# Masks on VectorE, casts off GpSimd, a written-out order for the first stages, DMA transposes of the last local q and k, and a last store in halves

## The chip, the cores and the metric

The kernel runs on one core of one Trainium2 chip. A core has TensorE (matrix products and transposes, which write PSUM), VectorE, ScalarE and GpSimd, and 16 DMA engines that are fed by queues on SyncE (SP) and GpSimd. Each engine works through its own instructions strictly in the order in which the program wrote them, and waits for other engines by semaphores. The metric is the device time of one execution in microseconds (us).

## The reference

Two layers, one after the other. The first is an attention over 8 batches, 8 heads, 576 positions and 64 columns a head:

```python
scores = scale * (q @ k.T)                   # per batch and head
mask_local   = (rel >= 0) & (rel < 32)       # heads 0 to 3, rel = row - column
mask_strided = (rel >= 0) & (col % 32 == row % 32)   # heads 4 to 7
attn = softmax(where(mask, scores, -1e9)); x = attn @ v   # -> [4608, 512]
```

The second is a feed-forward layer on the 4608 rows of x:

```python
h = x @ w_in                                 # [4608, 512] @ [512, 2048]
g = maximum(h, 0) + alpha * minimum(h, 0)    # alpha: one value a column
out = g @ w_out                              # [4608, 2048] @ [2048, 512]
```

All inputs and the output are float32; inside, the kernel works in float16 with float32 sums.

## The kernel before

**Attention.** The masks leave few scores alive, so only blocks are computed. Heads go in pairs, four pairs to a batch: pairs 0 and 1 (called a, b here) are local, six windows of 96 rows against 128 keys; pairs 2 and 3 (A, B) are strided, eight groups of 72 rows. The work of a pair is cut into pieces. **T** (`transpose_piece`, line 233) turns q or k of two pairs on TensorE, eight 128x128 transposes into PSUM, and ScalarE (for batches 0 and 1 ScalarE and VectorE) copies the result into `qT`, `kT`. **S** (`score_both`, line 388; `score_early` and `score_piece` for batches 0 and 1) computes the scores in two halves, i = 0 and 1; ScalarE takes the exponential into a tile `et`, and the mask is applied. **P** (`pv_piece`, line 435) multiplies with v, where a column of ones gives the softmax's sum; VectorE takes the reciprocal (line 458) and scales (line 460). **X** (`x_piece`, `x_dma`, `x_copy`) turns the result into `xT`, a ring of three batches.

**Masks.** For batches 0 and 1 an additive mask `madd` is added to the scores by a matrix product with the identity, before the exponential (lines 320 and 366). From batch 2 on the exponential is multiplied by a 0/1 mask on GpSimd (lines 423 and 430).

**Local q and k** come as float32, are cast by `cast_l` (GpSimd for batches 0 to 2, ScalarE for 3 to 7) and turned on TensorE. Strided q and k of batches 2 to 7 are turned by DMA transposes from `qsd`, `ksd` (`transpose_d`, line 132, on SP's queue).

**Feed-forward.** Rows go in nine chunks of 512 (n = 0 to 8). `lin1_piece(n, m)`, line 619, makes 128 of the 2048 columns: four products, then ScalarE's `neg` (line 639) and VectorE's combination into `gT` (line 641). It uses one of three PSUM buffers `hps`, so TensorE can run only three pieces ahead of VectorE. Chunk 0 uses the plain second product (`lin2_piece`, line 740). Chunks 1 to 8 use `fast_piece` (line 674), a two-by-two scheme with seven products P1 to P7, each in two pieces; it needs sums of quarters of `gT` (`g_sums`, on VectorE, line 647) and of `w_out` (`w_sums`). The last product, P3, completes a quadrant of 256 rows by 256 columns, which one addition and one store write out.

**Order.** Batch 0 runs alone at the start, between dummy products `warm` that keep TensorE busy. Then come the sixteen lin1 pieces of chunk 0, then its sixteen lin2 pieces with batch 1's attention pieces between them, and then chunks 1 to 8: each has 16 lin1 and 14 fast pieces, and attention pieces of a later batch are put between them, by the list `PACE1` for chunk 1 and by an even share for the others. The second half of a pair's exponentials is held back (`defer`) and issued one attention step later. GpSimd's queue carries all loads with a cast, in program order with its masks, casts and copies; SP's queue carries the stores, the later loads of local q and k, and all DMA transposes.

Of the kernel before, what the change touches and what calls it, by code (L numbers as in the profile page):

```python
# [31 lines left out]
def kernel(  # L32
# [21 lines left out]
    SUM1 = {8.5: [0], 18.5: [2], 19.0: [1, 3, 5], 20.5: [4], 22.0: [7], 24.5: [6]}  # L54
    PACE1 = (0, 1, 0, 0, 1, 0, 1, 0, 0, 0, 1, 1, 0, 1, 0, 1, 1, 1, 1, 2, 1, 1, 2, 0, 1, 2, 0, 1, 1, 1)
    SUMS = {10: [(0, LOW)], 16: [(1, LOW)], 17: [(0, HIGH)], 18: [(1, HIGH)],
            20: [(2, LOW)], 21: [(2, HIGH)], 23: [(3, LOW)], 25: [(3, HIGH)]}

# [49 lines left out]
    def load_qk(b, strided, nm):  # L108

        h0 = 4 if strided else 0
        src = q if nm == "q" else k
        if strided and b:
            t16 = hpool.tile([128, 2, 512], F16, tag=f"{nm}s", bufs=2, name=f"{nm}s")
            cast16[(b, True, nm)] = t16
        else:
            t16 = hpool.tile([128, 2, 512], F32, tag=f"{nm}l", bufs=2, name=f"{nm}l")
            loaded[(b, strided, nm)] = t16
        base = src[b, h0 : h0 + 1, 0:1, :]  # L120
        eng = nc.sync if (b > 2 and not strided) or (b == 0 and strided) else nc.gpsimd
        keep(eng.dma_start(t16, bass.AP(
            tensor=base.tensor, offset=base.offset,
            ap=[[8 * D, 64], [2 * S * D, 2], [S * D, 2], [1, 8 * D]])))
# [13 lines left out]
    def cast_s(b, nm, eng):  # L138
        t16 = hpool.tile([128, 2, 512], F16, tag=f"{nm}s", bufs=2, name=f"{nm}s")
        if eng[0] == eng[1]:  # L140
            cast_copy(eng[0], t16, loaded[(b, True, nm)])
        else:
            for f in range(2):
                cast_copy(eng[f], t16[:, f : f + 1, :], loaded[(b, True, nm)][:, f : f + 1, :])
        cast16[(b, True, nm)] = t16
# [20 lines left out]
    def load_v(b, strided):  # L166
# [8 lines left out]
        else:  # L175
            v16 = vls[b % 2]
            base = v[b, 0:1, 0:1, :]
            r0 = 32 if b < 2 else 0
            keep(nc.gpsimd.dma_start(
                v16[r0:128, :, 0:64],  # L180
                bass.AP(tensor=base.tensor, offset=base.offset - (32 - r0) * D,
                        ap=[[D, 128 - r0], [96 * D, 24], [1, D]])))
# [18 lines left out]
    def over_v(b, eng):  # L201

        v16 = vls[b % 2]
        cast_copy(eng, v16[0:32, 1:24, :], v16[96:128, 0:23, :])
# [6 lines left out]
    wide = {"on": True}  # L211
    NEARLY = 2

# [19 lines left out]
    def transpose_piece(u, nm):  # L233
# [6 lines left out]
        early = b < NEARLY  # L240
        src = cast16[(b, strided, nm)]
# [12 lines left out]
        if early:  # L254
            for e in range(2):
                eng = "dve" if (nm == "q") == (e == 0) else "act"
                if u == 0 and nm == "q":
                    eng = "act"
# [5 lines left out]
        if nm == "k":  # L264
            tails(b, u, strided)

    def tails(b, u, strided):
# [11 lines left out]
        qeng = "dve" if b < NEARLY else "act"  # L279
        for i, (o, eng) in enumerate(((qTs[u % 2][:, :, 0:576], qeng), (kTs[u % 2][:, :, 32:608], "act"))):  # L280
# [9 lines left out]
    def score_early(P):  # L290
# [3 lines left out]
        for i in range(2):  # L294
# [8 lines left out]
            n = w * len(grp)  # L303
            for x, t in enumerate(grp):
                k0 = 32 + 72 * t if P.strided else 96 * t
                for y in range(2):
# [3 lines left out]
                        P.qT[hf, w * t : w * t + w], start=(x == 0), stop=False, skip_group_check=True))  # L310
                    P.et[(2 * (t // 2) + y, t % 2) if P.strided else (t, y)] = (et, n * y + w * x)
            todo.append((i, et[0:r, 0 : 2 * n], sps, n))
        for i, ev, sps, n in todo:
            if not P.strided and i == 0:
                m = madd[:, 0:288]
            else:
                m = madd[0:72, 288:360] if P.strided else madd[:, 96:192]
                m = m.unsqueeze(1).to_broadcast([r, n // w, w])
            for y in range(2):
                keep(nc.tensor.matmul(  # L320
                    sps[y][:, 0:n], ident[0:r, :], m, start=False, stop=True, skip_group_check=True))
            if i == 0:
                keep(nc.scalar.activation(
                    ev.rearrange("r (y c) -> r y c", y=2), sp[0:r, :, 0:n], AF.Exp, scale=SCALE))
                continue
            for y in range(2):
                keep(nc.scalar.activation(
                    ev[:, n * y : n * y + n], sps[y][0:r, 0:n], AF.Exp, scale=SCALE))

    def score_piece(P, i):  # L330

        et = ets[ectr["i"] % NE]
        if wide["on"] and ectr["i"] % 2:
            sps = [phpool.tile([128, 512], F32, tag="hps", name="sph") for _ in range(2)]
        else:
            sp = pbpool.tile([128, 2, 512], F32, tag="sp", name="sp")
            sps = [sp[:, y] for y in range(2)]
        ectr["i"] += 1
        w, grp = P.w, P.sgroups[i]
        n = w * len(grp)  # L340
        r = 72 if P.strided else 128
        early = P.b < NEARLY
        for x, t in enumerate(grp):
            if P.dx:
                q0 = k0 = 80 * (4 * (2 * P.pr + t % 2) + t // 2)
            else:
                q0, k0 = w * t, 32 + 72 * t if P.strided else 96 * t
            for y in range(2):
                hf = slice(64 * y, 64 * y + 64)
                keep(nc.tensor.matmul(  # L350
                    sps[y][:, w * x : w * x + w], P.kT[hf, k0 : k0 + 128],
                    P.qT[hf, q0 : q0 + w], start=(x == 0),
                    stop=(x == len(grp) - 1 and not early), skip_group_check=True))

                key = (2 * (t // 2) + y, t % 2) if P.strided else (t, y)
                P.et[key] = (et, n * y + w * x)
        first = not P.strided and i == 0
        if early:

            if first:  # L360
                m = madd[:, 0:288]
            else:
                m = madd[0:72, 288:360] if P.strided else madd[:, 96:192]
                m = m.unsqueeze(1).to_broadcast([r, n // w, w])
            for y in range(2):
                keep(nc.tensor.matmul(
                    sps[y][:, 0:n], ident[0:r, :], m, start=False, stop=True, skip_group_check=True))
        ev = et[0:r, 0 : 2 * n]
        if wide["on"] and ectr["i"] % 2 == 0:
            for y in range(2):  # L370
                keep(nc.scalar.activation(
                    ev[:, n * y : n * y + n], sps[y][0:r, 0:n], AF.Exp, scale=SCALE))
        else:
            keep(nc.scalar.activation(
                ev.rearrange("r (y c) -> r y c", y=2), sp[0:r, :, 0:n], AF.Exp, scale=SCALE))
        if early:
            return
        if first:
            ev = ev.rearrange("r (y c) -> r y c", y=2)
            m = mfirst.unsqueeze(1).to_broadcast([r, 2, n])  # L380
        else:
            ev = ev.rearrange("r (c f) -> r c f", f=w)
            m = (mstr if P.strided else mother).unsqueeze(1).to_broadcast([r, 2 * n // w, w])
        keep(nc.gpsimd.tensor_tensor(ev, ev, m, op=ALU.mult))
# [3 lines left out]
    def score_both(P):  # L388

        w, r = P.w, 72 if P.strided else 128  # L390
        for i in range(2):
# [28 lines left out]
            if i == 0:  # L420
                keep(nc.scalar.activation(  # L421
                    ev.rearrange("r (y c) -> r y c", y=2), sp[0:r, :, 0:n], AF.Exp, scale=SCALE))
                keep(nc.gpsimd.tensor_tensor(mv, mv, m, op=ALU.mult))  # L423
                continue

            def ex(y):
                keep(nc.scalar.activation(  # L427
                    ev[:, n * y : n * y + n], sps[y][0:r, 0:n], AF.Exp, scale=SCALE))
                if y:
                    keep(nc.gpsimd.tensor_tensor(mv, mv, m, op=ALU.mult))  # L430
# [34 lines left out]
    def x_piece(P):  # L465
# [5 lines left out]
        if P.strided:  # L471
            keep(nc.scalar.copy(  # L472
                xT[:, P.hp, base : base + S].rearrange("r (p t) -> r p t", t=8),
                xp[:, 0:576].rearrange("r (t p) -> r p t", t=8)))
        else:
            cast_copy("act" if P.b < NEARLY and P.hp == 0 else "dve",
# [11 lines left out]
    def x_copy(P):  # L488
        base = (P.b % 3) * S
        keep(nc.scalar.copy(  # L490
            xT[:, P.hp, base : base + S].rearrange("r (p t) -> r p t", t=8),
            P.xs[:, :, 0:72].rearrange("r t p -> r p t")))
# [11 lines left out]
    def Sc(g, i):  # L504
        return lambda: score_piece(pairs[g], i)

# [5 lines left out]

    def alone(u0, u1):

        A, L = (2 * u0, 2 * u0 + 1), (2 * u1, 2 * u1 + 1)

        def Sb(g):
            return lambda: score_early(pairs[g])

        if u0 == 1:  # L520
            fns = [T(u0, "q"), T(u0, "k")] + [Sc(g, i) for g in A for i in range(2)]
            fns += [Pv(A[0], 0), T(u1, "q"), Pv(A[0], 1), T(u1, "k"), Pv(A[0], 2), Sc(L[0], 0), Sc(L[0], 1)]
            fns += [Pv(A[1], 0), Sc(L[1], 0), Pv(A[1], 1), Sc(L[1], 1), Pv(A[1], 2)]
        else:
            fns = [T(u0, "q"), T(u0, "k"), Sb(A[0]), Sb(A[1])]
            fns += [Pv(A[0], 0), T(u1, "q"), Pv(A[0], 1), T(u1, "k"), Pv(A[0], 2), Sb(L[0])]
            fns += [Pv(A[1], 0), Pv(A[1], 1), Sb(L[1]), Pv(A[1], 2)]
        fns += [Pv(L[0], 0), X(A[0]), Pv(L[0], 1), X(A[1])]
        fns += [Pv(L[1], 0), Pv(L[1], 1), X(L[0]), X(L[1])]
        for fn in fns:  # L530
            feed(fn, -1)

    alone(1, 0)
# [140 lines left out]
    def fast_piece(n, i):  # L674
# [25 lines left out]
        if tb == 0:  # L700
            return
# [247 lines left out]
```

## Time and profile before

| what | us |
|---|---|
| median of three runs | 323.99 (321.32 to 325.52) |
| the profiled execution | 322.7 |
| its span, first to last instruction | 320.5 |
| batch 0 and start, until lin1 of chunk 0 | 0 to 31.9 |
| lin1 of chunk 0 | 31.9 to 45.5 |
| lin2 of chunk 0 with batch 1 | 45.5 to 70.4 |
| chunk 1 | 70.4 to 108.7 |
| chunks 2, 3, 4, 5, 6 | 31.5, 31.6, 31.6, 30.7, 29.8 |
| chunk 7, no attention | 26.3 |
| chunk 8 and end | 290.2 to 320.5 |

The spans of the stages are read from the chain of waits, at the first lin1 product of each chunk. Times count from the span's start. In the profile's lists a row names the line, the engine, the operation, what it writes and reads (out<-in), the shape and the count; then follow the busy time, the mean of one in ns, and the engine's idle time before it with what ended it. PE is TensorE, PEld its weight loads, DVE VectorE, ACT ScalarE, POOL GpSimd, SP SyncE.

### The profile page before, as it was taken

The numbers are of one execution on the slowest core, as the hardware profiler recorded it, in microseconds if no ns is written. First come the engines' busy times: TensorE is split into PE (matmuls) and PEld (weight loads), VectorE is DVE, ScalarE is ACT, GpSimd is POOL, SyncE is SP. The second block draws the span as 40 slices with busy tenths as digits, with TensorE's granted clock in tenths as the row PEclk, the third lists the DMA queues.
The fourth block names the chain that finished last, engine by engine and source line by source line (L and its number), as shares of the span: only waits on it lengthen the run. The fifth ranks groups of instructions, "written<-read, shape, count | busy, mean of one in ns | idle before, by whom it ended". The sixth has DMA issues, their size and how long they took to land.

```text
span 320.5 us, 7312 instructions
## 1 busy us (share of the span) xinstructions
PE 304.7 (95%) x2925; PEld 203.5 (63%) x2925; DVE 240.1 (75%) x446; ACT 193.1 (60%) x353; POOL 127.6 (40%) x134
## 2 busy tenths in 40 slices
PE   6799998999888899999999999999999999999995
PEld 2355455555477547888886478548876884585484
DVE  5436785747987689868986897789788987947862
ACT  1355655539864876687668766877667446524630
POOL 8672299155494444444444434443423300000000
PEclk9669999999999999999999999999999999999999
DMA  7999999969978995599559946963631031002012
GB/s 216 202 206 206 231 183 148 170 69 213 154 159 124 239 151 88 101 246 149 82 109 229 165 67 112 203 70 50 130 108 20 18 90 65 2 33 100 0 35 98
DMA packets 81553, 40.39 MB, mean 126 GB/s; under 512 B 58464, under 2 KB 77168, under 8 KB 81520
## 3 DMA queue, kind: packets, MB, share of 16 engines
q0 software_dynamic: 41728, 17.38, 45.3%
q1 hardware_dynamic: 39792, 22.55, 31.6%
q8 instruction: 23, 0.38, 0.5%
q14 instruction: 10, 0.08, 0.1%
HBM read 38.01 MB, written 9.44 MB: 148 GB/s over the span
## 4 chain that ended last, share of the span: by engine, by line
PE 78%; DVE 7%; ACT 6%; DMA 6%; issue 2%; SPq 0%; ACTq 0%
PE hps L629 33%; PE fX L696 8%; PE fZ L696 8%; PE fY L696 8%; DMA kT<-ksd 4%; PE pv L451 4%; PE ops L762 3%; PE wps L784 2%; DMA kl<-in_k_dram 2%; PE fV L696 2%; DVE sg L647 2%; PE tp L247 2%; ACT xT L490 2%; PE sp L408 2%; DVE gT L641 2%
## 5 line engine op out<-in xcount | busy, mean ns | idle before, releaser
L629 PE MATMUL hps<-xT,win 128*128 128x512 f16 (+2 forms) x704 | 133.3, 340 | 2.1 <-ACT xT L472 0.7
L641 DVE SCALAR_TENSOR_TENSOR gT<-neg,oma,hps 128x512 f16<-128x512 f32 x144 | 104.3, 744 | 29.0 <-ACT neg L639 22.4
L639 ACT ACTIVATE neg<-hps 128x512 f32<-128x512 f32 x144 | 85.7, 600 | 40.4 <-PE hps L629 40.1
L629 PEld LDWEIGHTS <-win 128*128 128x128 f16 x704 | 63.4, 98 | 58.1 <-issue 4.5
L423 POOL TENSOR_TENSOR et<-et,consts 128x576 f16<-128x576 f16 (+1 forms) x24 | 30.6, 1274 | 93.7 <-ACT et L421 93.7
L696 PEld LDWEIGHTS <-sg 128*128 128x128 f16 x512 | 47.3, 98 | 5.8
L696 PEld LDWEIGHTS <-gT 128*128 128x128 f16 x384 | 35.7, 98 | 5.3
L460 DVE TENSOR_TENSOR x<-pv,rc 96x384 f16<-96x384 f32 (+2 forms) x62 | 33.0, 532 | 2.1
L430 POOL TENSOR_TENSOR et<-et,consts 128x576 f16<-128x576 f16 (+1 forms) x24 | 31.2, 1302 | 5.5 <-ACT et L427 4.7
L696 PE MATMUL fY<-wt,sg 128*128 128x256 f16 x256 | 32.3, 273 | 0.0
L696 PE MATMUL fX<-wout,gT 128*128 128x256 f16 x256 | 31.8, 273 | 0.0
L458 DVE RECIPROCAL rc<-pv 72x6 f32<-72x6 f32 (+2 forms) x80 | 14.6, 183 | 21.6 <-PE pv L451 21.4
L451 PEld LDWEIGHTS <-et 72*128 72x128 f16 (+1 forms) x448 | 24.3, 99 | 7.5 <-issue 0.5
L647 DVE TENSOR_TENSOR sg<-gT 128x1024 f16<-128x1024 f16 x32 | 21.8, 696 | 0.0
L421 ACT ACTIVATE et<-sp 128x576 f16<-128x576 f32 (+1 forms) x24 | 15.5, 645 | 8.7 <-PE sp L408 8.6
L784 PE MATMUL wps<-wrm 128*128 128x512 f16 x44 | 17.8, 478 | 1.2 <-DVE wrm L796 1.2
L427 ACT ACTIVATE et<-sph 128x288 f16<-128x288 f32 (+1 forms) x48 | 18.9, 408 | 0.0
L647 DVE TENSOR_TENSOR sg<-sg,gT 128x1024 f16<-128x1024 f16 x16 | 18.5, 1157 | 0.3
L696 PE MATMUL fZ<-wt,gT 128*128 128x256 f16 x128 | 16.3, 273 | 0.0
L762 PE MATMUL ops<-wout,gT 128*128 128x512 f16 x64 | 16.3, 379 | 0.0
L696 PE MATMUL fZ<-wt,sg 128*128 128x256 f16 x128 | 16.3, 272 | 0.0
L696 PE MATMUL fV<-wout,sg 128*128 128x256 f16 x128 | 16.1, 273 | 0.0
(110 smaller groups left out, 333.5 us busy)
## 6 DMA issues: line engine op xcount, KB each, us to landing
out_dram<-o SPq DMA_DIRECT2D x24, 256.0 KB, 2.7
ql<-in_q_dram SPq DMA_DIRECT2D x6, 512.0 KB, 5.7
kl<-in_k_dram SPq DMA_DIRECT2D x6, 512.0 KB, 7.7
stv<-in_v_dram POOLq DMA_DIRECT2D x8, 288.0 KB, 8.2
vl<-in_v_dram POOLq DMA_DIRECT2D x6, 384.0 KB, 8.4
win<-in_moe_w_in_dram POOLq DMA_DIRECT2D x4, 512.0 KB, 9.1
wout<-in_moe_w_out_dram POOLq DMA_DIRECT2D x4, 512.0 KB, 13.8
out_dram<-oc SPq DMA_DIRECT2D x8, 256.0 KB, 4.3
```

What stands on the lines that cost most here:

```text
L423: keep(nc.gpsimd.tensor_tensor(mv, mv, m, op=ALU.mult))
L427: keep(nc.scalar.activation(ev[:, n * y : n * y + n], sps[y][0:r, 0:n], AF.Exp, scale=SCALE))
L430: keep(nc.gpsimd.tensor_tensor(mv, mv, m, op=ALU.mult))
L451: keep(nc.tensor.matmul(pv[:, 65 * x : 65 * x + 65], et[0:r, c : c + 128], v16[0:r, 2 * P.pr + hh, t, :] if P.strided else v16[:, 6 * (2 * ...
L460: keep(nc.vector.tensor_tensor(P.x16[0:w, c0 : c0 + 64 * nb].rearrange("r (c e) -> r c e", e=64), pvv[:, :, 0:64], rc[0:w, 0:nb].unsqueeze ...
L629: keep(nc.tensor.matmul(hps[:, dst : dst + w], win16[:, kk, 128 * m : 128 * m + 128], xT[:, kk, src : src + w], start=(kk == 0 and x == 0) ...
L639: keep(nc.scalar.activation(neg, hps, AF.Relu, scale=-1.0))
L641: keep(nc.vector.scalar_tensor_tensor(gTs[n][:, m, :], neg, oma[:, m : m + 1], hps, op0=ALU.mult, op1=ALU.add))
L647: keep(eng.tensor_tensor(o, x, y, op=op))
L696: keep(nc.tensor.matmul(z[:, 256 * tb : 256 * tb + 256], x[:, p, 128 * tb : 128 * tb + 128], y[:, p], start=(opens and p == 0 and tb == 0) ...
L762: keep(nc.tensor.matmul(ops, gTs[n][:, kf, 128 * mt : 128 * mt + 128], wout16[:, kf, :], start=(kf == 0), stop=(kf == 15)))
L784: keep(nc.tensor.matmul(wps, wrm[:, 0:128], wrm, start=True, stop=True))
```

## The change

- From batch 1 on, the 0/1 mask is multiplied on VectorE. Batch 0 keeps the additive mask on TensorE; batch 1 loses its sixteen mask products; the 48 masks of batches 2 to 7 move from GpSimd to VectorE.
- The start, chunk 0 and batch 1 are written as one list of steps, `FIRST`, with a table of engines, `ENG`. GpSimd issues the loads of batches 0, 1 and 2 without casts between them, apart from batch 0's two local casts and one copy. Batch 1's strided v is cast on VectorE, its local q and k on ScalarE (before the scores of its strided pairs), and its `over_v` copy is on VectorE. The constants come in two transfers, the identity first, and batch 0's strided k is issued after both. Batch 0's order of pieces is otherwise that of before.
- `turn_l`: local q and k of batches 5, 6 and 7 are turned by two DMA transposes on SP's queue (128x1024 float16 each), issued with the step that follows their casts; ScalarE then copies them from SBUF into `qT`, `kT` instead of from PSUM. The short `tails` stay on TensorE.
- `x_copy` reads in order and writes with a step, where it read with a step and wrote in order.
- `SUM1` and `PACE1` of chunk 1 have other values; the number of pieces in chunk 1 (22) is the same.
- In chunk 8, P3's two pieces are each added and stored by themselves.

```diff
-    SUM1 = {8.5: [0], 18.5: [2], 19.0: [1, 3, 5], 20.5: [4], 22.0: [7], 24.5: [6]}
-    PACE1 = (0, 1, 0, 0, 1, 0, 1, 0, 0, 0, 1, 1, 0, 1, 0, 1, 1, 1, 1, 2, 1, 1, 2, 0, 1, 2, 0, 1, 1, 1)
+    SUM1 = {7.5: [0], 16.0: [2], 19.0: [1], 20.5: [3, 5], 21.5: [7], 23.0: [4], 24.5: [6]}
+    PACE1 = (0, 0, 1, 0, 1, 0, 1, 0, 0, 1, 0, 1, 1, 0, 0, 2, 0, 0, 2, 0, 3, 2, 0, 1, 2, 1, 1, 0, 2, 0)
+    FIRST = """
+        Mw Mq Mx Dq.0s Di Dc Dk.0s Da Dt.0s Dq.0l Dk.0l Mt.0 Mt.1 Me Dt.0l Dv.0s Mv.0 Dv.0l
+        w.12 id md cq.0s0 cq.0s1 ck.0s0 ck.0s1 T.0sq w.4 ap T.0sk w.4
+        S.0A0 w.1 S.0A1 w.1 cv.00 cv.01 S.0B0 w.1 S.0B1 w.1 cq.0l P.0A0 w.1 T.0lq w.1 P.0A1 w.1 ck.0l T.0lk w.1 P.0A2 w.1
+        Wi.0 Wi.1 Wi.2 Wi.3 Mv.1 vo.0 Wo.0 Wo.1 Wo.2 Wo.3
+        Dq.1s Dk.1s Dt.1s Dv.1s Dq.1l Dk.1l Dt.1l Dv.1l
...
+        Dq.2l Dk.2l Dt.2l Dv.2l Dd.2 Dv.2s
+        1.0 1.1 1.2 1.3 1.4 1.5 1.6 1.7 1.8 1.9 1.10 1.11 1.12 1.13 1.14 1.15
+        2.0 ws.0 2.1 ws.1 cv.10 cv.11 T.1sq T.1sk 2.2 cq.1l ck.1l S.1A S.1B 2.3 ws.2 P.1A0 T.1lq 2.4 P.1A1 T.1lk
+        2.5 ws.3 vo.1 P.1A2 S.1a 2.6 P.1B0 P.1B1 2.7 ws.4 S.1b P.1B2 2.8 P.1a0 X.1A 2.9 ws.5 P.1a1 2.10 X.1B 2.11 P.1b0
+        2.12 cq.2l ck.2l P.1b1 2.13 X.1a 2.14 X.1b 2.15
+        """.split()
...
+    def masked(P, i, ev, n, eng):
...
+        keep(eng.tensor_tensor(mv, mv, m, op=ALU.mult))
...
+            if not on_pe:
+                masked(P, i, ev, n, nc.vector)
...
-                keep(nc.gpsimd.tensor_tensor(mv, mv, m, op=ALU.mult))
+                keep(nc.vector.tensor_tensor(mv, mv, m, op=ALU.mult))
...
+        if b >= LX:
+            dst = (qTs if nm == "q" else kTs)[u % 2][:, :, slice(0, 512) if nm == "q" else slice(32, 544)]
+            cast_copy("act", dst.rearrange("r e (p t) -> r t p e", t=8),
+                      turned.pop(nm).rearrange("r (t p e) -> r t p e", t=8, e=2))
...
+    def turn_l(b):
+        for nm in "qk":
+            o = hpool.tile([128, 2, 512], F16, tag=f"{nm}s", bufs=2, name=f"{nm}x")
+            turned[nm] = o.rearrange("r a c -> r (a c)")
+            keep(nc.sync.dma_start_transpose(
+                turned[nm].rearrange("r (t c) -> r t c", c=128),
+                cast16[(b, False, nm)].rearrange("p t f d -> p (t f d)")))
...
-            xT[:, P.hp, base : base + S].rearrange("r (p t) -> r p t", t=8),
-            P.xs[:, :, 0:72].rearrange("r t p -> r p t")))
+            xT[:, P.hp, base : base + S].rearrange("r (p t) -> r t p", t=8), P.xs[:, :, 0:72]))
...
+                    if g % 4 == 1 and LX <= c + 1 < B:
+                        turn_l(c + 1)
...
+        if last and name == "P3":
+            h = slice(256 * tb, 256 * tb + 256)
+            r0 = 512 * n + 128 * tb
+            sub(nc.vector, cur["22"][:, h], z[:, h], cur["22"][:, h], ALU.add)
+            keep(nc.sync.dma_start(out[r0 : r0 + 128, 256:512], cur["22"][:, h]))
+            return
```

In `FIRST`, M is a memset, D a load (q, k, t for the tails, v, d for the strided pair before a DMA transpose), W a part of the weights, c a cast, vo the `over_v` copy, T, S, P and X the pieces above with the batch's number, 1 and 2 a lin1 and a lin2 piece, ws a part of `w_sums`, and w.n means n dummy products.

## The prediction

> **What bounds the kernel now.** I read the page's busy times first, then the chain of waits, then the stages in windows, then the timeline where TensorE stands.
>
> ```profile
> PE 304.7 (95%) x2925; PEld 203.5 (63%) x2925; DVE 240.1 (75%) x446; ACT 193.1 (60%) x353; POOL 127.6 (40%) x134
> ...
> PE 78%; DVE 7%; ACT 6%; DMA 6%; issue 2%; SPq 0%; ACTq 0%
> ```
>
> TensorE is busy 95% of the span and holds 78% of the chain, so a change pays where it takes work from TensorE, or where TensorE stands still. The windows (us, then busy us of TensorE, weight loads, VectorE, ScalarE, GpSimd, then clock, DMA and GB/s) show where that is:
>
> ```profile
> 45.50:70.40 24.90, 23.43 (x260) 13.96 (x259) 16.10 (x36) 11.86 (x26) 13.22 (x14) 1.00 0.92 132
> 70.40:88.00 17.60, 16.70 (x135) 8.21 (x134) 13.43 (x23) 15.71 (x30) 10.11 (x9) 1.00 1.46 179
> 88.00:108.70 20.70, 17.79 (x234) 14.73 (x233) 16.37 (x31) 12.84 (x25) 12.75 (x13) 1.00 0.90 142
> 171.80:187.00 15.20, 15.13 (x113) 7.21 (x113) 12.69 (x22) 11.43 (x21) 5.46 (x6) 1.00 1.23 201
> 187.00:203.40 16.40, 16.26 (x204) 13.91 (x203) 13.54 (x28) 11.29 (x22) 8.41 (x8) 1.00 0.56 95
> ```
>
> The last two are chunk 3, lin1 part and fast part: TensorE idles 0.2 us in 31.6. Chunk 1 (rows two and three) idles 3.8 us, lin2 of chunk 0 1.5 us. The largest single stall of chunk 1 is this, in the timeline:
>
> ```profile
> 92.33 3.38 DVE L647 TENSOR_TENSOR sg<-sg,gT 128x1024 f16<-128x1024 f16 x1
> ...
> 97.06 0.23 PE L247 MATMUL tp<-consts,kl 128*128 128x128 f16 x1 [2.05 <-DVE x16s L460]
> ```
>
> The same sum takes 0.68 us wherever GpSimd computes nothing beside it. Here two GpSimd masks (92.62 to 95.15) lie over it, the scaling at 96.45 behind it is late, and TensorE waits 2.05 us for a PSUM buffer. In all, the seven `sg<-sg,gT` sums that meet GpSimd work take 12.3 us, where the nine others take 0.68 each: 7.5 us of VectorE lost.
>
> **The change part by part.** The sum is made against the profiled execution, 322.7 us (span 320.5, 2.2 around it); the median, 323.99, stands 1.3 higher, and the answer is moved by that.
>
> **1. Start, 0 to 31.9: 0.0 (-0.6 to +0.6).** Batch 0's pieces, engines and mask products are as before. SP issues one more transfer before strided k: 0.58 to 0.61 us an issue. The chain begins with k's landing at 9.36, but behind it VectorE's cast took 1.10 against 0.62 on ScalarE for an equal half, while GpSimd cast until 10.2; a k that lands 0.5 later meets less of that. Sixteen lin1 pieces of chunk 0: nothing changes.
>
> **2. Lin2 of chunk 0 with batch 1: -0.9 (-2.4 to +0.8).** Sixteen mask products of 288 columns go. A lin1 product of 512 columns takes 0.219 (13.77 us for 63), so 288 take 0.12: 1.9 us of TensorE. In the first half, until 57.5, TensorE waits for exponentials (0.73, 0.49 and 0.11 idle in `score_early`), and `cq.1l`, `ck.1l` now stand before them in ScalarE's queue: 2 x 1.06 = 2.1 us (rows of `ql<-ql`, `kl<-kl`). Laid from the start of lin2 on: ScalarE ends its copies at 3.9, the casts at 6.0, the first exponential at 6.6, where it ended at 6.2 before (51.66). What the eight strided mask products give is waited away. In the second half no idle over 0.06 us is left, and eight products x 0.12 = 0.96 come off. GpSimd no longer casts there; `wt` at 46.98 took 1.33 instead of 0.68 beside such a cast, but nothing waited for it. Both ends: all mask time and half of the idle comes off, or VectorE's masks, which wait for ScalarE, hold back the copies that the local scores need.
>
> **3. Chunk 1: -2.7 (-4.0 to -0.8).** No mask on GpSimd is left there. The stalled sums return to 0.68 and the 2.05 us go. The last piece, whose X feeds chunk 2, comes one fast piece (1.04) earlier in `PACE1`, which covers the 0.71 us that TensorE waited for `xT` at 108.70. Together 2.76. The 0.65 us before the strided scores (they wait for `kT`'s DMA transpose, landed 87.53) stay: both lists reach that piece in step 15, and the lin1 part has ScalarE busy 15.7 of 17.6 us. VectorE in the fast part: 16.4 busy, less 2.7 for the sums, plus eight masks at 0.45 (below): 17.3 in about 18. That is close, hence the lower end.
>
> **4. Masks of chunks 2 to 6 on VectorE: +0.8 (-1.0 to +3.5).** No mask on VectorE is in the trace. Rows: 1024 float16 with two inputs 0.68 us; from PSUM 384 elements 0.553 and 256 0.421, so 1.03 ns an element and 0.16 fixed. With 0.16 fixed, the 1024 row gives 0.51 ns an element: 576 cost **0.45**. At the full 1.03 they cost 0.75. I take 0.45, the row of the same type and place; lower bound 0.38 (0.68 x 576/1024). Eight a chunk add 3.6 us; the sums give about 1.0 back (1.64 at 188.31 for 0.68): VectorE goes from 26.2 to 28.8 of 31.6. In the lin1 part two scores put four masks (1.8 us) on VectorE's 12.7 of 15.2. They queue among the combinations that free `hps`, and TensorE runs three buffers ahead. A later 0.6 us sum in chunk 7 at 274.77 cost it 0.14 idle; four such a chunk would be 0.5, half of it hidden under the scores' own 0.5 us on TensorE and in shorter waits of P: 0.16 x 5.
>
> **5. Transfers for q and k of batches 5 to 7: -2.4 (-2.7 to +1.5).** Eight transposes hold the chain 0.45 us (125.77 and 128.15): 6 x 0.45 = 2.7 off TensorE. Added on SP: six DMA transposes. A pair of larger ones (`qT<-qsd`, `kT<-ksd`) takes 1.3 and 1.8 us to issue and lands 5.7 us after the first issue when little else runs (227.58 to 233.28), 7 to 9 beside loads. For batch 5 the step is at 173.8, the casts end at 172.7, and one `xT` transpose is ahead at 176.1: landing about 185; T is due at 188.75 and 191.12. SP's next item is a transpose at 185.3, so none waits. ScalarE's copies cost 1.02 from PSUM; from SBUF they are unseen. `x_copy` before, which stepped through SBUF, took 1.30 for 576 against 0.64 from PSUM, so 1.0 to 2.3 each. With 2.3, ScalarE gains 7.7 us over three fast parts that have 5 us free each. I take 0.1 us lost a batch. `x_copy` itself costs between 0.64 and 1.30, no more than now.
>
> The Trainium skill speaks against this copy: "SBUF — State Buffer", section "Door 1: The DMA port swizzle", says that SBUF is accessed in lines of 16 bytes and that each access that crosses to a new line pays. The 1.30 row agrees for reads; the new copies write with a step of exactly 16 bytes, so by the page they are at the 2.3 end, `x_copy` gains nothing, and the sum here would be nearer -2.0.
>
> **6. The end: -0.5 (-0.2 to -0.9).** Now the addition takes 0.69 at 316.62, the store is issued at 317.34 and lands 2.2 later. The half takes 0.42 (row 256 elements): -0.27; half the bytes, -0.2.
>
> Loads: GpSimd issues batch 2's without casts between (before, `qsd` was issued at 51.42 behind four of them), but TensorE never waited for those.
>
> Sum: 0.0 - 0.9 - 2.7 + 0.8 - 2.4 - 0.5 = **-5.7**. 322.7 - 5.7 = 317.0 profiled, 318.3 as a median. A measurement of this kernel tells about 2%, 6.5 us: the line is at 317.5.
>
> **Rivals.**
> *Further ahead* (30%): chunk 8 without attention takes 26.3 like chunk 7, chunks 2 to 4 take 31.5; their attention has some 11100 columns, 4.7 us at 512 in 0.219, so 0.5 us a chunk is waiting that the modelled ends hide. If short masks (1.27 to 0.45) remove it, 5 x 0.5 = 2.5 and the 0.8 go: 318.3 - 3.3 = 315.0. For it: 93.7 us of GpSimd's idle time ends with an exponential. Against: TensorE's idle there is already under 0.3.
> *Transposes late* (16%): SP's `kT<-ksd` took 5.83 us to issue and 12 to land at 75.53, beside 1 MB of loads. If those of batches 5 and 6 land after 189, ScalarE stands in order before seeds and exponentials: 2 x 2 us, and the 2.7 hardly show: 318.3 + 3.5 = 321.8.
> *VectorE becomes the bound* (12%), the slower side: at 0.75 a mask, eight are 6.0, and 26.2 + 6.0 - 1.0 = 31.2 of 31.6 us. An in-order engine that waits for exponentials is not filled over 95%: 32.8 a chunk, +1.3 x 5 = 6.5; part 5 gains nothing then (2.4), chunk 1 loses half (1.4), and the 0.8 is in it: 318.3 + 6.5 + 2.4 + 1.4 - 0.8 = 327.8. It decides from (0.95 x 31.6 - 25.2)/8 = 0.60 us a mask. Against: the 0.68 row.
> *The change doing nothing* in part 5 (T's time merely turns into ScalarE's) is inside the second.
>
> **How the numbers follow.** Forecast 42%, 316 to 320.5; a third of it and more, 15 points, lies under 317.5. Faster 0.30 + 0.15 = 0.45; slower by over 2% (330.5) a third of the last rival, 0.05; within 2% 0.50. The range goes from 313 (the first rival's lower part left out, 7 points) to 325 (most of the last, 9 points).
>
> **What would show it.** Masks near 0.45 us on VectorE; no `sg` sum over 0.8; chunk 1 near 35.6 us; lin2 of chunk 0 near 24.0; chunks 2 and 3 within 0.3 of before, 4 to 6 (where T falls) shorter by 0.8; the end 0.5 shorter. It is wrong if VectorE's masks wait for exponentials while combinations stand behind them, or if ScalarE's copy of turned q waits for a DMA.

## The result, and the profile after

| kernel | us, median of all runs | ratio to before, 95% interval |
|---|---|---|
| before, same comparison | 324.38 (321.32 to 325.52) | |
| after | 349.14 (347.90 to 354.91) | 1.077 (1.067 to 1.086): slower |

The forecast was 318.3, the range 313 to 325, and slower by over 2% had a chance of 0.05. The time rose by 25 us instead. Medians here and below are of all executions, while ratios leave out those over 1.5% above the kernel's fastest; of one kernel below (`LX` = 8) only the execution of 327.03 us is left, so it has no interval.

The profiled execution took 347.9 us, its span 346.1. Stage by stage, each from the first lin1 product of a chunk to that of the next, in us (these borders lie up to 1.5 us ahead of those in the table of before, which were read from the chain of waits):

| | start | chunk 0 | 1 | 2 | 3 | 4 | 5 | 6 | 7 | 8 and end |
|---|---|---|---|---|---|---|---|---|---|---|
| before | 31.4 | 38.8 | 36.9 | 32.1 | 31.6 | 31.5 | 31.5 | 29.8 | 26.4 | 30.4 |
| after | 29.8 | 40.6 | 36.3 | 32.0 | 39.8 | 40.3 | 39.0 | 29.8 | 27.7 | 30.9 |

Of 25.6 us more, 24.5 are in chunks 3, 4 and 5, the ones in which q and k of batches 5, 6 and 7 are turned. (The prediction is one off there: it looks for this in chunks 4 to 6, and the windows that it calls chunk 3, 171.8 to 203.4, are chunk 4. Chunks 3 to 5 of before are alike, so no number hangs on it.) The engine sums of the page:

```profile
PE 306.6 (89%) x2861; PEld 203.3 (59%) x2861; DVE 252.5 (73%) x507; ACT 223.7 (65%) x355; POOL 61.1 (18%) x81
```

TensorE's busy time is no smaller, 306.6 for 304.7, although 64 products left, and its share fell from 95 to 89%. ScalarE is up by 30.6 us. The chain of waits of this page breaks off at the last store, so the stages are read from windows, cut at this kernel's own borders (lin2 of chunk 0; chunk 1, two rows; chunk 3, lin1 and fast part; columns as before):

```profile
43.40:70.40 27.00, 23.36 (x246) 13.44 (x244) 20.95 (x48) 13.91 (x29) 10.49 (x12) 0.94 1.51 136
70.40:88.00 17.60, 16.64 (x119) 7.93 (x117) 14.50 (x26) 15.65 (x29) 5.80 (x6) 1.00 1.49 169
88.00:106.70 18.70, 17.16 (x245) 14.96 (x246) 15.63 (x39) 13.56 (x24) 5.55 (x8) 1.00 1.43 216
138.70:154.00 15.30, 14.69 (x160) 11.61 (x158) 13.63 (x26) 11.54 (x20) 3.27 (x4) 1.00 1.20 210
154.00:178.50 24.50, 18.37 (x210) 15.20 (x210) 14.44 (x33) 19.42 (x22) 1.81 (x3) 0.86 0.74 78
```

The last row answers to this one, chunk 3's fast part of before:

```profile
154.60:170.90 16.30, 16.30 (x209) 14.32 (x207) 13.77 (x29) 11.19 (x22) 8.84 (x9) 1.00 0.56 93
```

It takes 24.5 us where it took 16.3. TensorE, which never idled there, now stands for 6.1 us, and the granted clock is 0.86: products that took 16.30 us take 18.37. The timeline shows both (start, length, engine, line, operation, and in brackets the idle time before it with what ended it):

```profile
157.84 4.76 ACT L213 COPY qT<-qx 128x1024 f16<-128x1024 f16 x1
...
162.89 4.70 ACT L213 COPY kT<-kx 128x1024 f16<-128x1024 f16 x1
...
167.65 0.42 PE L410 MATMUL sp<-qT,kT 64*128 64x96 f16 x6 [5.53 <-ACT kT L213]
...
168.24 1.89 PE L670 MATMUL fY<-wt,sg 128*128 128x256 f16 x8
```

ScalarE copies the turned q and then k for 9.5 us; TensorE's local scores stand in order behind them. Eight products of 256 columns, which take 1.04 at full clock (161.07, say), then take 1.89. The groups, with shapes apart, name the instructions (first of after, then of before):

```profile
L492 ACT COPY xT<-xs 128x576 f16<-128x576 f16 x6 | 16.5, 2758 | 0.0
...
L213 ACT COPY qT<-qx 128x1024 f16<-128x1024 f16 x3 | 14.2, 4747 | 0.0
L213 ACT COPY kT<-kx 128x1024 f16<-128x1024 f16 x3 | 14.0, 4680 | 0.0
```

```profile
L490 ACT COPY xT<-xs 128x576 f16<-128x576 f16 x6 | 7.8, 1304 | 0.0
```

Both new forms write with a step: `x_copy` of 16 bytes, the turned copies of 16 bytes within each of two halves between which they alternate (the prediction, which has "exactly 16 bytes" for both, leaves the halves out). So no two writes in a row go to neighbouring places. They take 4.7 us where I had bounded 1.0 to 2.3, and 2.76 where I had written "no more than now".

### The profile page after: what moved, and what is told of

It is laid out like the page before. It is cut to its first block, busy times and chain, and to the rows that moved or that the text cites. A ratio compares the mean times of both kernels' runs of the same rounds, so it can differ in the third digit from the quotient of the medians.

```text
span 346.1 us, 7130 instructions
## 1 busy us (share of the span) xinstructions
PE 306.6 (89%) x2861; PEld 203.3 (59%) x2861; DVE 252.5 (73%) x507; ACT 223.7 (65%) x355; POOL 61.1 (18%) x81
## 5 line engine op out<-in xcount | busy, mean ns | idle before, releaser
L670 PEld LDWEIGHTS <-sg 128*128 128x128 f16 x512 | 49.5, 102 | 9.2 <-issue 1.3
L670 PE MATMUL fY<-wt,sg 128*128 128x256 f16 x256 | 34.8, 286 | 0.0
L670 PE MATMUL fX<-wout,gT 128*128 128x256 f16 x256 | 31.6, 273 | 0.0
L425 DVE TENSOR_TENSOR et<-et,consts 128x576 f16<-128x576 f16 (+1 forms) x24 | 10.8, 452 | 24.2 <-ACT et L423 24.1
L410 PE MATMUL sp<-qT,kT 64*128 64x72 f16 (+1 forms) x168 | 7.6, 208 | 17.4 <-ACT kT L213 16.6
L410 PEld LDWEIGHTS <-kT 64*128 64x128 f16 x336 | 7.6, 99 | 24.5 <-ACT kT L213 17.8
L205 POOL DMA_DIRECT2D vl<-in_v_dram x8 | 11.4, 1428 | 51.2 <-PE pv L453 46.4
L429 ACT ACTIVATE et<-sph 128x288 f16<-128x288 f32 (+1 forms) x48 | 20.3, 441 | 0.0
L158 POOL DMA_DIRECT2D qsd<-in_q_dram x6 | 4.5, 750 | 83.3 <-DMA qT<-qsd 83.3
L670 PE MATMUL fZ<-wt,sg 128*128 128x256 f16 x128 | 18.9, 300 | 0.0
L764 PE MATMUL wps<-wrm 128*128 128x512 f16 x44 | 16.6, 454 | 1.2 <-DVE wrm L785 1.2
```

What stands on the lines that cost most here:

```text
L410: keep(nc.tensor.matmul(sps[y][:, w * x : w * x + w], P.kT[hf, k0 : k0 + 128], P.qT[hf, q0 : q0 + w], start=(x == 0), stop=(x == len(grp) ...
L429: keep(nc.scalar.activation(ev[:, n * y : n * y + n], sps[y][0:r, 0:n], AF.Exp, scale=SCALE))
L670: keep(nc.tensor.matmul(z[:, 256 * tb : 256 * tb + 256], x[:, p, 128 * tb : 128 * tb + 128], y[:, p], start=(opens and p == 0 and tb == 0) ...
L764: keep(nc.tensor.matmul(wps, wrm[:, 0:128], wrm, start=True, stop=True))
```

## The experiments

**1. Three kernels that each take one suspect away.** The theory: the copies' writes with a step are slow. The rival: the transfers come late, or load the queue.

`turn_off`:

```diff
-    LX = 5
+    LX = 8
```

> The changed kernel with batches 5 to 7 turned on TensorE again (LX = 8): no turned transfer, no stepped copy of q and k; all else as changed, x_copy's stepped write too. Theory (ScalarE's copies that write with a step of 16 bytes cost 4.7 us each; TensorE then waits 5.5 us for kT and runs at half clock behind it): chunks 3, 4 and 5, which took 39.8, 40.3 and 39.0, come back to 31.5 to 32.5, so 349 becomes 323 to 327. Rival 'transfers' (SP's and the DMA engines' extra work is the price): the same here. Rival 'masks on VectorE': nothing comes back, over 340.

`turn_read_step` (the same elements to the same places; only the order in which ScalarE walks over them changes, so the step, 256 bytes, is on the read side):

```diff
-            cast_copy("act", dst.rearrange("r e (p t) -> r t p e", t=8),
-                      turned.pop(nm).rearrange("r (t p e) -> r t p e", t=8, e=2))
+            cast_copy("act", dst.rearrange("r e (p t) -> r e p t", t=8),
+                      turned.pop(nm).rearrange("r (t p e) -> r e p t", t=8, e=2))
```

> The changed kernel with the six DMA transposes kept, but ScalarE's copy of turned q and k reads with a step (256 bytes) and writes in order. Theory: the write step is the price; a read with a step cost 1.30 us for 576 elements in x_copy before, so 2.3 us for 1024; TensorE's wait for kT falls from 5.5 to below 1 us and its clock stays full: 325 to 331. Rival 'transfers': still over 340, because the transposes are all there. Rival 'any step through SBUF costs the same': the copies stay at 4 to 5 us and the time at 345 to 352.

`xcopy_old` (`x_copy` as in the kernel before, the rest as changed):

```diff
-            xT[:, P.hp, base : base + S].rearrange("r (p t) -> r t p", t=8), P.xs[:, :, 0:72]))
+            xT[:, P.hp, base : base + S].rearrange("r (p t) -> r p t", t=8),
+            P.xs[:, :, 0:72].rearrange("r t p -> r p t")))
```

> The changed kernel with x_copy as before (reads with a step of 160 bytes, writes in order), nothing else. Theory: x_copy goes from 2.76 back to 1.30 us, six times; TensorE's idle time at the chunk ends (0.6 to 0.7 before X and 0.6 to 0.7 before lin1, 1.2 before chunk 7) mostly goes: 5 to 9 us less, 340 to 345. If x_copy is hidden: within 2 us of 349.

| kernel | us | ratio | chunks 3, 4, 5 | 7 |
|---|---|---|---|---|
| `turn_off` | 333.06 (327.03 to 334.04) | | 32.9, 32.8, 32.9 | 27.7 |
| `turn_read_step` | 327.37 (325.45 to 328.72) | 1.023 (1.011 to 1.035) | 32.5, 32.4, 32.4 | 27.7 |
| `xcopy_old` | 341.12 (339.68 to 344.98) | 1.064 (1.053 to 1.075) | 39.1, 38.3, 38.0 | 26.4 |

With all transfers in place and only the order of the copies turned round, 21.8 us of the 25 are gone by the medians, and in the profiles chunks 3 to 5 together fall from 119.1 to 97.2 us. Here are the copies of `turn_read_step`, and its first local scores, which now wait 0.18 us where they had waited 5.53:

```profile
L213 ACT COPY qT<-qx 128x1024 f16<-128x1024 f16 x3 | 6.0, 2016 | 0.0
L213 ACT COPY kT<-kx 128x1024 f16<-128x1024 f16 x3 | 6.0, 2009 | 0.0
```

```profile
162.74 0.30 PE L410 MATMUL sp<-qT,kT 64*128 64x96 f16 x6 [0.18 <-ACT kT L213]
```

That refutes the transfers as the cause of the loss. In the changed kernel's trace those of batch 5 had landed at 154.36 and 157.93, and ScalarE's copies (157.84 and 162.89) began without a DMA wait. `x_copy` alone is worth 1.3 us in chunk 7 and, over chunks 3 to 5 of `xcopy_old`, 3.7; half clock (TensorE at half of its full clock) lasts 3.4 us longer in those chunks of `xcopy_old` than in the changed kernel's, which makes the 3.7 a low figure. The median of `turn_off` missed 323 to 327: in its profile half clock holds for 13.7 us at the start and 6.8 in chunk 0. Its chunks 3 to 5 came back to 32.9 each, 0.4 above what I expected.

**2. The price of a step.** `probe_steps` is the kernel before with fourteen copies behind the end, which leave the output as it is: eight of ScalarE, three each of VectorE and GpSimd, in order or with a step on one side. In short:

```diff
+    keep(nc.scalar.copy(stepped(pd, 1024, 1), stepped(ps_, 1024, 1)))
+    keep(nc.scalar.copy(stepped(pd, 1024, 2), stepped(ps_, 1024, 1)))
...
+    keep(nc.gpsimd.tensor_copy(stepped(pd, 1024, 1), stepped(ps_, 1024, 8)))
```

> The kernel before with fourteen copies of float16 from SBUF to SBUF after its end, one after the other, which measure the disputed cost by itself: ScalarE 1024 elements with a write step of 1, 2, 4 and 8 elements and 512 with a step of 16, then with a read step of 2, 4 and 8; VectorE and GpSimd with no step, a write step of 8 and a read step of 8. Theory: ScalarE with a write step of 8 takes 4.6 to 4.8 us, with 1 about 1.05, and a read step of 8 about 2.3; it rises between 4 and 8. Rival 'the copies in the kernel are slow from other traffic': a write step of 8 takes under 2.5 us here, where nothing else runs. The time of the whole kernel is before's plus some 30 us.

ScalarE's rows in the timeline: a plain copy, writes with steps of 2, 4 and 8 float16 and 512 elements with a step of 16; then reads with steps of 2, 4 and 8:

```profile
317.23 1.04 ACT L927 COPY wt<-win 128x1024 f16<-128x1024 f16 x1 [0.72 <-PE fY L696]
318.30 1.34 ACT L928 COPY wt<-win 128x1024 f16<-128x1024 f16 x1
319.68 2.46 ACT L929 COPY wt<-win 128x1024 f16<-128x1024 f16 x1
322.17 4.71 ACT L930 COPY wt<-win 128x1024 f16<-128x1024 f16 x1
326.91 2.33 ACT L931 COPY wt<-win 128x512 f16<-128x512 f16 x1
329.27 1.04 ACT L932 COPY wt<-win 128x1024 f16<-128x1024 f16 x1
330.35 1.09 ACT L933 COPY wt<-win 128x1024 f16<-128x1024 f16 x1
331.47 1.99 ACT L934 COPY wt<-win 128x1024 f16<-128x1024 f16 x1
```

With steps of 4, 8 and 16 bytes, 1024 writes touch 256, 512 and 1024 stretches of 16 bytes and take 1.34, 2.46 and 4.71: 4.4 ns for each further stretch, and beyond 16 bytes no more an element (512 in 2.33). I had expected the rise only between 8 and 16 bytes. Reads are different: next to nothing up to 8 bytes, 1.99 at 16. The Trainium skill ("SBUF — State Buffer", section "Specifications (TRN2)") says that lines are 16 bytes, that each cross to a new line pays, and that full bandwidth needs at least two hits a line. For reads two hits do (1.09 for 1.04 in order). For writes they don't: two hits cost 2.46, and one hit over twice what a read pays, which is what decided here. GpSimd shows the same pair (4.71 and 1.97 for 1.04), VectorE 2.43 and 1.07 for 0.43.

**3. What the wait costs beside its own length.** The theory says that a slow chunk's 8 us are the wait of 5.5 us and the half clock behind it. `fill_gap` puts 24 products of dummy data in front of the first local scores of batches 5 to 7; the kernel is otherwise as changed.

```diff
+        if P.b >= LX and P.hp == 0:
+            fill = pspool.tile([128, 512], F32, tag="ps", name="fill")
+            for _ in range(24):
+                keep(nc.tensor.matmul(fill, wrm[:, 0:128], wrm, start=True, stop=True))
```

> The changed kernel with 24 dummy products of 512 columns (5.25 us of TensorE) put before the first local scores of batches 5, 6 and 7, where TensorE waits 5.5 us for kT. ScalarE's copies are as slow as before. Theory on the clock (half speed for 3.4 or 6.8 us comes after an idle stretch): no half speed at these three places, products behind the gap at 1.04 us for eight instead of 1.9, 1.7 to 3.4 us less a chunk: 339 to 345. Rival: the low clock has another cause; it stays, and the time is 348 to 352.

It took 345.55 us (345.26 and 345.83), a ratio of 1.081 (1.069 to 1.093) in its comparison: just outside what I expected. By the ratios, this one and the changed kernel's 1.077 (1.067 to 1.086), the two kernels can't be told apart; the profiles show what happens at the three places. A window over the gap and what follows, of the changed kernel and of `fill_gap`:

```profile
167.60:175.00 7.40, 7.35 (x76) 5.70 (x77) 4.70 (x12) 3.44 (x9) 0.00 (x0) 0.68 0.81 122
```

```profile
160.00:175.00 15.00, 14.63 (x138) 10.56 (x137) 8.08 (x21) 13.10 (x12) 0.00 (x0) 1.00 0.44 50
```

The clock behind the gap is 0.68 with the wait and 1.00 with it filled, and chunks 3 to 5 of `fill_gap` have no half clock at all. They take 37.8, 37.7 and 37.7 us for 39.8, 40.3 and 39.0: half clock cost 5.9 us in all. The wait itself is 5.5 three times, 16.6. Both make 22.5, close to the 21.9 that `turn_read_step` took out of these chunks.

**4. The change with both copies mended.** `fixed` has the diffs of `turn_read_step` and `xcopy_old` together; `fixed_whole` also stores the last quadrant in one piece; `masks_alone` is the kernel before with nothing but the 48 masks of batches 2 to 7 on VectorE.

```diff
-        if last and name == "P3":
+        if False and name == "P3":
```

```diff
-                keep(nc.gpsimd.tensor_tensor(mv, mv, m, op=ALU.mult))
+                keep(nc.vector.tensor_tensor(mv, mv, m, op=ALU.mult))
```

> The changed kernel with both copies in the order that reads with a step and writes in order (turned q and k, and x_copy as before); everything else as changed. Theory (the two write steps are the whole loss against before): chunks 3 to 5 near 30.7 us, which is 31.5 less the 0.9 of turned transposes plus little; chunk 2 31.2; 318 to 323, level with before or up to 3 us under it. If the loss has a further part (transfers, masks, casts on ScalarE): above 326.

> The same with the last quadrant stored whole again. The trace of the changed kernel shows TensorE idle 1.08 us before P3's second piece, until VectorE has added the first. Theory: the halves cost more than they save; without them the end is 0.4 to 0.8 us shorter (30.9 to 30.4). Rival: the earlier store is worth 0.5 as forecast, and this is 0.5 longer.

> The kernel before with one edit: the 48 masks of batches 2 to 7 on VectorE. Theory: the masks cost nothing that shows; the 2.05 us stall of chunk 1 goes and a chunk loses no time: 1 to 3 us under before. Rival 'masks': VectorE's queue delays the combinations, 2 us or more over before.

| kernel | us | ratio | start | chunk 0 | 1 | 2 | 3 | 4 | 5 | 8 and end |
|---|---|---|---|---|---|---|---|---|---|---|
| before, here | 322.54 (317.39 to 325.95) | | 31.4 | 38.8 | 36.9 | 32.1 | 31.6 | 31.5 | 31.5 | 30.4 |
| `fixed` | 320.38 (317.97 to 323.75) | 1.003 (0.997 to 1.008) | 32.2 | 41.8 | 33.9 | 31.2 | 31.1 | 31.0 | 31.0 | 30.9 |
| `fixed_whole` | 321.21 (318.41 to 325.08) | 1.003 (0.999 to 1.008) | 30.4 | 41.1 | 36.8 | 31.2 | 31.1 | 31.4 | 31.0 | 30.5 |
| `masks_alone` | 318.16 (317.12 to 320.06) | 0.996 (0.991 to 1.001) | 28.1 | 39.2 | 35.5 | 32.1 | 31.5 | 31.5 | 31.5 | 30.4 |

(The stages of before are those of the first profile.) The mended change can't be told from the kernel before. Against `masks_alone`, chunks 3 to 5 of `fixed` show what leaving T out is worth: 0.5 each. Its three chunks take 93.1 us where `turn_read_step` takes 97.2, so the stepped write of `x_copy` cost them 4.1. Chunk 1 can't be read from one profile: `fixed` and `fixed_whole` have the same instructions there and take 33.9 and 36.8. The masks cost VectorE 0.45 us each and the chunks nothing. Of `masks_alone`:

```profile
L430 DVE TENSOR_TENSOR et<-et,consts 128x576 f16<-128x576 f16 x12 | 5.4, 453 | 2.4 <-ACT et L427 2.1
...
L423 DVE TENSOR_TENSOR et<-et,consts 72x576 f16<-72x576 f16 x12 | 5.4, 448 | 1.0 <-ACT et L421 1.0
```

The store in halves costs 0.4 in the profile, too little for the run times to tell. The changed kernel's timeline at the end:

```profile
341.48 0.43 DVE L621 TENSOR_TENSOR o<-fV,o 128x256 f32<-128x256 f32 x1
341.96 1.03 PE L670 MATMUL fV<-wout,sg 128*128 128x256 f16 x8 [1.08 <-DVE o L621]
```

TensorE's second half of `fV` waits 1.08 us for VectorE's addition of the first half, which reads the same PSUM tile. In one piece both halves run back to back (1.91 us). A tile for each half wasn't tried.

**5. Chunk 0.** It is 1.8 to 3.6 us longer than before in the changed kernel and in the forms so far. In the timeline of `fixed`, ScalarE does batch 1's two casts between the strided scores and their exponentials:

```profile
51.54 1.08 ACT L213 CAST ql<-ql 128x1024 f16<-128x1024 f32 x1
51.61 0.30 PE L362 MATMUL sp<-qT,kT 64*128 64x72 f16 x8 [1.36 <-ACT kT L213]
52.48 1.08 ACT L213 CAST kl<-kl 128x1024 f16<-128x1024 f32 x1
53.43 0.66 ACT L379 ACTIVATE et<-sp 72x576 f16<-72x576 f32 x1
54.15 0.42 PE L362 MATMUL sp<-qT,kT 64*128 64x72 f16 x8 [2.10 <-ACT et L379]
```

TensorE waits 1.36 and 2.10 us, where it had waited 0.73 and 0.49 before, and runs at half clock for 6.8 us from 53.9 on. But before isn't always so. `probe_steps`, whose chunk 0 has the same instructions, took 42.2 there, with half clock for 6.8 us, and `masks_alone` 39.2, with a first wait of 1.10. The first wait in before and in `probe_steps`:

```profile
50.19 0.30 PE L308 MATMUL sp<-qT,kT 64*128 64x72 f16 x8 [0.73 <-ACT kT L187]
```

```profile
50.02 0.30 PE L308 MATMUL sp<-qT,kT 64*128 64x72 f16 x8 [1.88 <-ACT kT L187]
```

So the 1.8 to 3.6 us have no firm size. The second wait has: 2.1 us in all seven profiles with the casts in front, at most 0.5 in the three with the chunk 0 of before. `fixed_casts_pool` gives the casts to GpSimd, `fixed_casts_late` leaves them on ScalarE but behind both scores; `best` has the casts on GpSimd, the strided transposes ahead of VectorE's `w_sums` and casts of v, a lin2 piece between the two scores, and the whole store.

```diff
-        Dq.2l Dk.2l Dt.2l Dv.2l Dd.2 Dv.2s
+        Dq.2l Dk.2l Dt.2l cq.1l ck.1l Dv.2l Dd.2 Dv.2s
...
-        2.0 ws.0 2.1 ws.1 cv.10 cv.11 T.1sq T.1sk 2.2 cq.1l ck.1l S.1A S.1B 2.3 ws.2 P.1A0 T.1lq 2.4 P.1A1 T.1lk
+        2.0 ws.0 2.1 ws.1 cv.10 cv.11 T.1sq T.1sk 2.2 S.1A S.1B 2.3 ws.2 P.1A0 T.1lq 2.4 P.1A1 T.1lk
```

> The kernel with both copies stepping on the read side, and batch 1's two local casts on GpSimd, issued ahead of the second batch's load of local v, instead of on ScalarE ahead of the strided scores. Theory (the casts stand before the exponentials in ScalarE's queue, so that TensorE waits 1.36 and 2.10 us at the start of lin2 and then runs at half speed for 6.8 us): the first wait stays, the second falls from 2.1 to 0.5 us or less, no half clock follows, chunk 0 (lin1 and lin2) takes 39 to 39.5 us instead of 41.8, and the whole is 1.5 to 3 us shorter. Rival (the longer chunk 0 comes from the order of the products, with the strided scores moved against the lin2 products, or from VectorE's casts, not from ScalarE's casts): chunk 0 stays at 41 or more, and the time within 0.5 us.

```diff
-        2.0 ws.0 2.1 ws.1 cv.10 cv.11 T.1sq T.1sk 2.2 cq.1l ck.1l S.1A S.1B 2.3 ws.2 P.1A0 T.1lq 2.4 P.1A1 T.1lk
+        2.0 ws.0 2.1 ws.1 cv.10 cv.11 T.1sq T.1sk 2.2 S.1A S.1B cq.1l ck.1l 2.3 ws.2 P.1A0 T.1lq 2.4 P.1A1 T.1lk
```

> The same kernel with both copies stepping on the read side, the two casts on ScalarE but issued after the two strided scores instead of before them. Theory (their place in ScalarE's queue is what costs): second wait 0.5 us or less, no half clock there, chunk 0 39 to 40 us; the casts may then hold back the local transposes, a wait of up to 1 us further on. Rival (it is the engine that counts, since 2.1 us of casts have to be done by ScalarE somewhere in the first half of lin2): a wait of 1.5 to 2 us appears a few us later, and chunk 0 stays at 41.

```diff
-        2.0 ws.0 2.1 ws.1 cv.10 cv.11 T.1sq T.1sk 2.2 cq.1l ck.1l S.1A S.1B 2.3 ws.2 P.1A0 T.1lq 2.4 P.1A1 T.1lk
+        2.0 2.1 T.1sq T.1sk ws.0 cv.10 cv.11 2.2 S.1A 2.3 S.1B ws.1 ws.2 P.1A0 T.1lq 2.4 P.1A1 T.1lk
```

> All that the runs so far point to together: masks on VectorE, transposes by transfer with both copies stepping on the read side, batch 1's local casts on GpSimd, the strided transposes of batch 1 and their scores each moved one lin2 product later or earlier so that TensorE has a product to do while it waits, and one whole last store. Theory: chunk 0 39 us, chunk 1 34 to 35, chunks 2 to 5 31.0, end 30.5: 314 to 317 us, ratio to the kernel before 0.975 to 0.99. Rival (what falls at one place turns up as a longer wait at another, since ScalarE and VectorE are the ones that are late): within 1 us of the kernel with both copies mended, 320.

| kernel | us | ratio | chunk 0 | waits of TensorE there | half clock there |
|---|---|---|---|---|---|
| before, here | 321.5 (316.55 to 324.48) | | 38.8 | 0.73, 0.49 | none |
| `fixed_casts_pool` | 319.97 (317.75 to 322.00) | 1.002 (0.996 to 1.007) | 40.8 | 2.30, 0.50 | 6.8 |
| `fixed_casts_late` | 319.50 (315.12 to 326.48) | 0.997 (0.990 to 1.004) | 41.1 | 2.27, 0.61 | 6.8 |
| `best` | 318.67 (314.98 to 323.50) | 0.992 (0.987 to 0.998) | 39.0 | 0.37, 1.19, 1.24, 0.52 | none |

My theory was half right. Without the casts in front the second wait does fall, from 2.10 to 0.5 and 0.6. But the first was 2.3, and the half clock stayed. The timeline of `fixed_casts_late` shows why:

```profile
46.67 1.67 DVE L215 COPY vs<-stv 72x1024 f16<-72x1024 f16 x2
48.26 0.68 DVE L215 COPY qT<-tp 128x512 f16<-128x512 f16 x1
```

```profile
50.22 0.30 PE L362 MATMUL sp<-qT,kT 64*128 64x72 f16 x8 [2.27 <-ACT kT L213]
```

VectorE casts batch 1's strided v before it copies the turned q, and ScalarE's copy into `kT` comes behind that. The two casts took 1.34 and 0.41 here, and 0.42 each in `fixed`. What lengthens them is in the traces. In five (`turn_read_step`, `xcopy_old`, `fill_gap`, `best` and this one) the first cast began while GpSimd was issuing a load (here 46.34 to 47.79), and each time it ended 0.22 to 0.23 us behind that issue, after 0.45, 0.64, 0.67, 1.16 and 1.34 us. In `turn_off` and `fixed_casts_pool` a cast on GpSimd was under way in the same manner, and one of the two took 1.26. And in all nine traces with this order of pieces TensorE's first wait is 1.36 us plus what the two casts take over 0.42 each, to within 0.11: 1.36 in `fixed`, 2.20 in `turn_off`, 2.27 here. So in `fixed_casts_late` the wait is long by where the load's issue fell, not by the edit; in `fixed_casts_pool` the GpSimd cast is one of the two that the edit put there. In `best` the casts of v come behind the copies and TensorE has products to do in between: the first wait is 0.37, the half clock doesn't come, and chunk 0 is back at 39.0. That is one execution: four of its twelve ran at a granted clock of 0.972 or 0.973, the profiled one at 0.992, so in those half clock came somewhere. `best` changes several places at once, so which of them did it isn't told apart. It missed my 314 to 317 and is 0.8% under before by its interval, the only one whose interval lies below 1; `masks_alone`, with two edited lines, can't be told from it.

## Why the prediction was wrong

**Part 5 failed, and it is the whole result.** The step was: "`x_copy` before, which stepped through SBUF, took 1.30 for 576 against 0.64 from PSUM, so 1.0 to 2.3 each", and "`x_copy` itself costs between 0.64 and 1.30, no more than now". The row of 1.30 steps on the read side; I scaled it to 1024 and took it as the upper end for a write. A read of 1024 with a step costs 1.99 to 2.02 (16 and 256 bytes), a write 4.71. With 4.7 the six copies add 3.7 each to ScalarE, 7.4 a batch against the 5 us that I had counted free, and they stand in one piece ahead of local scores that TensorE does in order. So where I had -2.4, chunks 3 to 5 grew by 24.5 us: 21.9 from the turned copies and 4.1 from `x_copy`, less 1.6 gained. `x_copy` cost another 1.3 in chunk 7. The point in the text from the skill went the right way, and stopped at the same 2.3.

**A term was missing**: what TensorE loses after a wait. 5.5 us of wait brought another 2.0 of half clock a chunk. The page of before showed it only at the start.

The other steps:

- **Part 1**, 0.0: 29.8 for 31.4 in the profiles. But the start alone runs from 28.1 to 33.7 us over the kernels, mostly with how long half clock lasts there (3.4 to 13.7 us), so it says nothing of the edit.
- **Part 2**, -0.9, became +1.8 in the changed kernel's profile (the chunk 0 of before took 38.8, 39.2 and 42.2 in three). The sixteen mask products went, and new waits took their place with half clock behind them. I had ScalarE's casts in the sum (first exponential 0.4 later), but laid them against the exponential alone: VectorE's casts of v ahead of `qT` weren't in it.
- **Part 3**, -2.7: the sums fell as forecast (`sg<-sg,gT` 685 ns on average for 1157). Chunk 1 gained 0.7 in the changed kernel and 0.0 to 3.0 in the other forms, with 2.9 between two profiles of the same instructions: the 2.05 us wait is gone, but at the end of the changed kernel's chunk TensorE waits 1.47 for an exponential of the last pair. The 0.71 us wait for `xT` falls in chunk 2 by the borders used here. It went as forecast in the forms that have `x_copy` as before (chunk 2 of `fixed` takes 31.2 for 32.1); in the changed kernel a wait of 0.60 at the end of chunk 2 stands against it.
- **Part 4**, +0.8: 0.45 a mask was right, and the cost nothing. The rival that VectorE becomes the bound fell: 0.45 is under its 0.60. The 95% in it was an assumption that no run tests: over any 31.6 us of the thirteen traces VectorE is at most 93% busy.
- **The transposes late**: they weren't. The rival had ScalarE standing behind them; ScalarE itself was late.
- **Further ahead** gave -0.5 a chunk for the masks; `masks_alone` gives 0.0 in chunks 2 to 5.
- **T's gain** without the slow copies is 0.5 a batch where I had 0.8.
- **Part 6**, -0.5, was +0.5. The half was costed as an addition and a store; that in this program the second half's products wait until the first half of the same tile has been read wasn't in it.

## What to carry to other kernels

A step has a side and a width: before an access pattern is turned round, take the price of a strided write from a row that writes. A copy on an engine in order is worth what stands behind it, and a wait of TensorE that is long enough costs a second time in clock: here 2.0 us for each 5.5. Before a tile is stored in halves, look whether the second half's products wait for the reading of the first: here they did, and it cost 0.4 us.

## What the runs showed of the hardware that I had not expected

- **Half clock comes on a grid.** In the changed kernel it starts at 11.89, 52.85, 165.49, 206.45 and 247.41 us and lasts 3.41 or 6.83: the distances are 12, 33, 12 and 12 times 3.413. The distances are whole numbers of 3.413 in the twelve other traces too, each with its own offset. This is what the Trainium skill says ("TensorE: Matmul & The Clock Gate", section "What's actually happening"): a free-running window of 3413 ns. It names an idle window as what starts half clock, but here a window need not be idle throughout: behind the start, every one at full clock in which TensorE idled 2.06 us or more brought it, none under 1.58 did, and of those between some did (1.58, 1.65, 1.88, 1.90) and some didn't (1.63, 1.69, 1.78, 1.83, 1.92, 1.97).
- **The clock goes with most of the spread of one kernel.** Before took 317.4 to 326.0 us over the 28 executions of one comparison. The eleven with a granted clock of 0.992 or more had spans of 315.4 to 318.3, the eleven at 0.979 or less 320.9 to 323.9. In the profiles of all kernels half clock at the start held from 3.4 us (start 28.1) to 13.7 (33.7); why it holds longer in one execution than in another wasn't tested.
